# Attention with normalised queries and keys, then a SoLU feed-forward: eleven weight combinations to VectorE, later inner sums, and another way of taking the moments of the last four tiles

## The chip, the cores and the metric

The kernel runs on one core of a Trainium2 chip. The metric is the device time of one execution in microseconds; lower is better. A core has TensorE (PE in the profile, with its weight loads as PEld), VectorE (DVE), ScalarE (ACT), GpSimd (POOL) and SyncE (SP, which here only issues DMAs). Each engine works through its own list of instructions in order, and semaphores make one wait for another.

## The reference

Two blocks follow each other. The attention block takes q, k, v of 8 batches, 12 heads, 448 positions and 64 columns; its result, reshaped to 3584 x 768, is the input x of the feed-forward block.

```python
q_n, k_n = (rmsnorm(q, g_q), rmsnorm(k, g_k))
scores = scale * np.matmul(q_n, k_n.transpose(0, 1, 3, 2))
scores = scores - np.max(scores, axis=-1, keepdims=True)
attn = np.exp(scores)
attn = attn / (np.sum(attn, axis=-1, keepdims=True) + 1e-09)
return np.matmul(attn, v).astype(np.float32)
...
h = x @ w_in
h_max = np.max(h, axis=-1, keepdims=True)
e = np.exp(h - h_max)
sm = e / (np.sum(e, axis=-1, keepdims=True) + 1e-09)
solu = h * sm
mu = np.mean(solu, axis=-1, keepdims=True)
var = np.mean((solu - mu) ** 2, axis=-1, keepdims=True)
ln = (solu - mu) / np.sqrt(var + 1e-06) * g_ln
return (ln @ w_out).astype(np.float32)
```

w_in is 768 x 1024, w_out 1024 x 768. The kernel computes in fp32; the weights reach it as doubles.

## The kernel before

**Three stages.** `fast_path` first runs attention in quads of four heads. Then comes the stage of `w_in`: x in 28 tiles of 128 rows, two tiles to a group `g`, 14 groups. Then the last stage: the normalised result times `w_out`, four tiles to a product, seven products. Both matrix products are made by a scheme of seven half-sized products instead of eight, for which sums and differences of the blocks of both factors are needed; in the last stage the scheme is applied twice, once to halves and once inside each of the seven products.

**The stage of `w_in`.** The seven products of a group are parts `p1` to `p7` (functions in `products`, L1100 the matmul, six matmuls each). They run in the order p6, p5, p7, p4, then p1 of the next group, p3, then p2 of the next group; 98 parts in all. p1, p6 and p7 add up in one PSUM bank, A; p5 and p3 in bank B; p2 has C and p4 has D. `part` (L1107) is ACT's copy of bank A, once after each of p1, p6, p7. `plus` (L1116) is DVE's drain of a bank: it adds ACT's copy, writes a quarter of `h` and carries the row maximum (`top`). So p3 may begin on bank B only when DVE has drained p5's and p7's sum from it, and p7 on bank A only when ACT has copied it.

For the next group POOL makes the block sums: L1076 and L1077 (`block_sums` part 0), then L1079 and L1080 (part 1; L1079 makes the operand of p7). L1076 waits for ACT's L1059 (`sizes`, which uses the same buffer first), and that for DVE's L1048 (`scale`).

**The steps of a tile.** When both halves of a tile's `h` are there (`done`: tile 2g+1 after p4, tile 2g after p3), these steps follow, each put some units of the schedule later (a unit is a part): the exponential on ACT (L1171); `ff_mult`, the product with `h` on DVE, for tiles 0 to 23 by an instruction that also sums the row (L1185, then the mean, L1186); `ff_deviations`, ACT's squares of the deviations from the mean (L1196); `ff_spread_of`, three [128,1] steps on POOL (L1201 to L1204) that end in `shift`; `ff_norm` on ACT (L1224); `ff_spread`, DVE's transpose (L1234) and four DMA stores on SP. For the last four tiles, 24 to 27, `ff_mult` is a plain product (L1180) and `ff_moments` takes mean and variance by batch-norm statistics on DVE (L1212, L1213, three small steps), with two small steps on POOL (L1218, L1220).

**Weights of the last stage.** During the stage of `w_in` the blocks of `w_out` are converted, and 44 subtractions (`combine`, L567, 128x384 each) make the combinations that the scheme needs. All stand on POOL, one per part from part 54 to part 89. They come in chains of four, `t3 = b22 - t1`, `t1 = t1 - b11`, `t2 = b22 - t1`, `t4 = b21 - t2`, so one of a chain may overwrite or read what the one before it touched.

**The seam.** Near the end of the stage the first operands of the last stage are made: tiles 0 to 3 come back from DRAM (`load_u`, SP, L1289), `make` puts them in place (`a11`, `s1`; later `s2`, `a12`, `s3`, ...), and `inner_sums` (four additions on POOL, L1330 to L1333) makes the sums for the inner scheme. PE's matmuls of the last stage are L1352; ACT's and DVE's drains there L1364, L1366, L1391, L1404, L1414.

**What sets the order.** The schedule is written by hand: `unit` emits a part and then what has come due, `follow(parts, i, f)` puts `f` behind part `i`, `later(n, f)` puts it `n` units on. Each engine's instructions stand in the order in which this code emits them.

Of the kernel before, what the change touches and what calls it, by code (L numbers as in the profile page):

```python
# [9 lines left out]
FP32 = mybir.dt.float32  # L10
# [4 lines left out]
OP = AluOpType  # L15
# [351 lines left out]
def fast_path(  # L367
# [24 lines left out]
    nc = tc.nc  # L392
    B, H, S, D = q.shape
    DM, DFF = moe_w_in.shape
    P = 128
# [9 lines left out]
    NG = NT // 2  # L405
# [8 lines left out]
    small = ctx.enter_context(tc.tile_pool(name="small", bufs=4))  # L414
# [8 lines left out]
    w_out = conv = sums_in = None  # L423
# [14 lines left out]
    mhalf = consts.tile([P, 1], FP32, name="mhalf")  # L438
# [121 lines left out]

    def combine(b, i):

        b11, b21, b22, t1, t3, t2, t4 = b
        o, p, q = [(t3, b22, t1), (t1, t1, b11), (t2, b22, t1), (t4, b21, t2)][i]
        nc.gpsimd.tensor_tensor(o, p, q, OP.subtract)  # L567

    def combine_in(x):
        c, i = divmod(x, 4)  # L570
        combine([w_in[k][:, c] for k in range(7)], i)

    def combine_out(x):

        if x < 16:
            k, i = divmod(x, 4)
            combine([w_out[:, a, (0, 3, 1, 2)[k]] for a in range(7)], i)
        else:
            a, i = divmod(x - 16, 4)
            combine([w_out[:, (0, 1, 5, 3, 4, 2, 6)[a], k] for k in range(7)], i)  # L580

    def load_again(x):

# [416 lines left out]
    mt = {}  # L1000
# [161 lines left out]
    def ff_max(t):  # L1162
        d = mt[t]
        d["nmax"] = small.tile([P, 1], FP32, tag="hmax", name="hmax")
        nc.vector.tensor_scalar(d["nmax"], d["top"], -1.0, None, OP.mult)
# [4 lines left out]
        d["s"] = small.tile([P, 1], FP32, tag="hsum", name="hsum")  # L1170
        nc.scalar.activation(d["u"], d["h"], AF.Exp, bias=d["nmax"], accum_out=d["s"])  # L1171

    def two_pass(t):
        return t < 2 * (NG - 2)

    def ff_mult(t):
        d = mt[t]
        u, h = d["u"], d["h"]
        if not two_pass(t):
            nc.vector.tensor_tensor(u, h, u, OP.mult)  # L1180
            return
        x = small.tile([P, 3], FP32, tag="um", name="um")
        total, mean, dev = x[:, 0:1], x[:, 1:2], x[:, 2:3]
        d["mean"], d["dev"] = mean, dev
        nc.vector.tensor_tensor_reduce(u, h, u, 1.0, 0.0, OP.mult, OP.add, total)  # L1185
        nc.vector.tensor_scalar(mean, total, -1.0 / DFF, None, OP.mult)  # L1186
        s = d["s"]
        e = d["e"] = small.tile([P, 1], FP32, tag="he", name="he")
        nc.gpsimd.tensor_scalar(s, s, 1e-9, None, OP.add)
        nc.gpsimd.tensor_scalar(e, s, s, 1e-6, OP.mult, OP.mult)  # L1190
# [7 lines left out]
    def ff_spread_of(t):  # L1198
# [3 lines left out]
        nc.gpsimd.tensor_tensor(e, e, mhalf, OP.pow)  # L1202
        d["shift"] = small.tile([P, 1], FP32, tag="shift", name="shift")
        nc.gpsimd.tensor_tensor(d["shift"], d["mean"], e, OP.mult)  # L1204

    def ff_moments(t):
        d = mt[t]
        u, s = d["u"], d["s"]
        bs = small.tile([P, 2, 6], FP32, tag="bs", name="bs", bufs=2)
        d["mv"] = small.tile([P, 2], FP32, tag="mv", name="mv", bufs=2)  # L1210
        for half in range(2):
            nc.vector.bn_stats(out=bs[:, half], in_=u[:, half * 512 : half * 512 + 512])  # L1212
        nc.vector.bn_aggr(out=d["mv"], in_=bs)  # L1213
        e = d["e"] = small.tile([P, 1], FP32, tag="he", name="he")
        nc.vector.tensor_scalar(s, s, 1e-9, None, OP.add)
        nc.vector.tensor_scalar(e, s, s, 1e-6, OP.mult, OP.mult)
        nc.vector.tensor_tensor(e, e, d["mv"][:, 1:2], OP.add)
        nc.gpsimd.tensor_tensor(e, e, mhalf, OP.pow)  # L1218
        d["shift"] = small.tile([P, 1], FP32, tag="shift", name="shift")
        nc.gpsimd.tensor_scalar(d["shift"], d["mv"][:, 0:1], e, -1.0, OP.mult, OP.mult)  # L1220

    def ff_norm(t):
        d = mt[t]
# [18 lines left out]
    def in_parts():  # L1242
        def done(g, i):
            t = 2 * g + i
            ff_max(t)
            waits = {
                (NG - 2, 1): (1, 2, 4, 6, 6), (NG - 2, 0): (2, 3, 5, 7.25, 8),
                (NG - 1, 1): (1, 2, 3.25, 6.75, 7.25), (NG - 1, 0): (2.25, 4.25, 7, 7.75, 8.75),
            }.get((g, i))
            if two_pass(t):  # L1250
                steps = (ff_exp, ff_mult, ff_deviations, ff_spread_of, ff_norm, ff_spread)
                waits = (1, 2, 3, 4, 5, 7) if i else (2, 3, 4, 6, 7, 9)
            else:
                steps = (ff_exp, ff_mult, ff_moments, ff_norm, ff_spread)
            for x, f in zip(waits, steps):
                later(x, lambda f=f: f(t))

        p = [products(g, lambda i, g=g: done(g, i)) for g in range(NG)]
        parts = [p[0][1], p[0][2]]
        for g in range(NG):  # L1260
            turn = [p[g][6], p[g][5], p[g][7], p[g][4], p[g][3]]
            x = len(parts)
            if g + 1 < NG:
                turn[4:] = [p[g + 1][1], p[g][3], p[g + 1][2]]
            parts += turn
# [55 lines left out]
    def inner_sums(n, name):  # L1321

        own = last.get("u", last["first"])
        a = us[n, name]
        sm = us[n, name, "sums"] = own.tile(
            [P, 4, KC, 4, 32], FP32, tag="sums", name="sums", bufs=2 if own is last["first"] else 4
        )
        a11, a12, a21, a22 = [a[:, t, k * KC : (k + 1) * KC] for t in range(2) for k in range(2)]
        s1, s2, s3, s4 = [sm[:, i] for i in range(4)]
        nc.gpsimd.tensor_tensor(s1, a21, a22, OP.add)  # L1330
        nc.gpsimd.tensor_tensor(s2, s1, a11, OP.subtract)
        nc.gpsimd.tensor_tensor(s3, a11, a21, OP.subtract)
        nc.gpsimd.tensor_tensor(s4, a12, s2, OP.subtract)  # L1333
# [112 lines left out]
    def follow(p, i, f):  # L1446
        g = p[i]

        def both():
            g()  # L1450
            later(1, f)

        p[i] = both
# [61 lines left out]
    with tc.manual_schedule():  # L1515
# [68 lines left out]
        for m in range(1, NQ):  # L1584
            a, b = 2 * m, 2 * m + 1
# [162 lines left out]
        w_out = pool(ctx, "w2", side="right").tile([P, 7, 7, KC, N2], FP32, name="w_out")  # L1748
# [19 lines left out]
        parts = in_parts()  # L1768
# [3 lines left out]
        for x in range(8):  # L1772
            follow(parts, 30 + 2 * x, lambda x=x: combine_out(x))
        for x in range(8, 44):
            follow(parts, 46 + x, lambda x=x: combine_out(x))
        follow(parts, 54, open_first)
        follow(parts, 3, lambda: load_sums(B - 1))
        follow(parts, 6, lambda: (invert(B - 1), send_inverses(B - 1)))
# [1 line left out]
        for name, t, h, i, j in (("a11", 0, (0,), 62, 66), ("a11", 1, (0,), 69, 73), ("s1", 2, (0, 1), 76, 82), ("s1", 3, (0, 1), 83, 89)):  # L1780
            follow(parts, i, lambda t=t, h=h: [load_u(0, t, x) for x in h])
            follow(parts, j, lambda name=name, t=t: make(0, name, t % 2))
        follow(parts, 89, lambda: inner_sums(0, "a11"))
        follow(parts, 93, lambda: inner_sums(0, "s1"))
        for p in parts:
            unit(p)

# [15 lines left out]
        for n in range(NS):  # L1803
            base = period * n
            for i, name in enumerate(ORDER):
                q = len(ORDER) * n + i
# [3 lines left out]
                x = HALVES[name][0]  # L1810
# [118 lines left out]
```

## Time and profile before

| what | before |
|---|---|
| median of 3 runs | 792.34 us (790.93 to 792.76) |
| the profiled execution | 791.55 us |
| its span, first to last instruction | 789.9 us |
| mean granted clock of TensorE | 0.999 |
| w_out subtractions (L567) on POOL | 44, 51.4 us, 1170 ns mean |

The profile is of one execution, so its rows add up to its own 789.9 us, not to the median. It names engines as above, lines of the kernel as L567, and writes an operation as output <- input. An idle time stands in brackets with the engine and line whose end released the instruction. A group of rows gives count, busy time and mean in ns.

### The profile page before, as it was taken

Reading aid. Unit: us, or ns where it says so; the run is one execution under the profiler, and the core shown is the slowest. Engines: PE = TensorE matmul, PEld = TensorE weight load, DVE = VectorE, ACT = ScalarE, POOL = GpSimd, SP = SyncE. Lnnn points to the kernel's source line nnn. Section 1 sums busy time; section 2 is a strip of 40 time slices with the busy share of each in tenths; the row PEclk is TensorE's granted clock in tenths of the full one; section 3 lists DMA queues with packets and bytes.
Section 4 is the critical chain, followed back from the end, with each engine's and each line's share of the span. In section 5 each row is a group of like instructions: output and inputs, shape, how many; then the busy total and the mean of one; then the engine's idle time right before and its main releaser. Section 6 shows DMA issues by size and latency. Waiting matters only on the chain.

```text
span 789.9 us, 15265 instructions
## 1 busy us (share of the span) xinstructions
PE 778.3 (99%) x5374; PEld 481.8 (61%) x5374; DVE 592.8 (75%) x1055; ACT 502.0 (64%) x825; POOL 483.0 (61%) x624
## 2 busy tenths in 40 slices
PE   8999999999999999999999999999999999999997
PEld 4444445444454544444444444443799999999996
DVE  6877997999898883687777666666897685866944
ACT  6776998887979763787777655554526445464410
POOL 2565344454354351455687688899887777867861
PEclk9999999999999999999999999999999999999999
DMA  8889898889898256577786666572757557357312
GB/s 174 177 183 202 172 207 185 187 193 187 169 199 188 77 154 165 141 191 182 186 203 171 166 152 157 138 200 54 210 151 255 162 186 258 127 201 236 105 61 85
DMA packets 279827, 134.28 MB, mean 170 GB/s; under 512 B 190332, under 2 KB 264892, under 8 KB 279740
## 3 DMA queue, kind: packets, MB, share of 16 engines
q1 hardware_dynamic: 265900, 123.31, 62.9%
q10 hardware_dynamic: 13840, 9.90, 4.4%
q8 instruction: 44, 0.72, 0.4%
q14 instruction: 43, 0.35, 0.2%
HBM read 96.12 MB, written 37.04 MB: 169 GB/s over the span
## 4 chain that ended last, share of the span: by engine, by line
PE 86%; POOL 8%; ACT 2%; issue 1%; DVE 1%; DMA 1%; SPq 0%; POOLq 0%; ACTq 0%; DVEq 0%
PE A L1352 16%; PE s L876 15%; PE o L888 15%; PE A L1100 10%; PE B L1352 8%; PE B L1100 6%; PE sm L948 4%; PE C L1352 4%; PE C L1100 3%; PE D L1100 3%; POOL w_out L567 3%; PE pt L790 1%; POOL he L1202 1%; POOL he L1201 1%; POOL xsum L1080 1%
## 5 line engine op out<-in xcount | busy, mean ns | idle before, releaser
L726 POOL TENSOR_TENSOR qkn<-qk,ny 128x896 f32<-128x896 f32 x45 | 77.2, 1735 | 113.9 <-DVE ny L720 82.0
L876 PE MATMUL s<-qkT 64*64 64x448 f32 x1288 | 139.4, 541 | 0.3 <-ACT qkT L742 0.2
L836 ACT ACTIVATE E<-s 128x896 f32<-128x896 f32 x144 | 124.4, 920 | 20.8 <-PE s L876 20.0
L888 PE MATMUL o<-E,v 64*64 64x448 f32 x1104 | 120.4, 536 | 0.0
L876 PEld LDWEIGHTS s<-qkT 64*64 64x64 f32 x1288 | 65.9, 191 | 60.1 <-issue 39.1
L1352 PE MATMUL A<-w_out,sums 128*128 128x192 f32 x392 | 79.9, 326 | 0.3 <-ACT u L1364 0.3
L1352 PE MATMUL B<-w_out,sums 128*128 128x192 f32 x392 | 79.8, 326 | 0.0
L1100 PE MATMUL B<-w_in,xsum 128*128 128x512 f32 x168 | 76.8, 593 | 1.2 <-DVE top L1116 1.2
L1100 PE MATMUL A<-w_in,xg 128*128 128x512 f32 x168 | 76.9, 593 | 0.8 <-POOL xg L1079 0.8
L888 PEld LDWEIGHTS o<-E,v 64*64 64x64 f32 x1104 | 42.3, 133 | 56.2 <-issue 51.5
L1352 PEld LDWEIGHTS A<-w_out,sums 128*128 128x128 f32 x392 | 66.3, 190 | 0.6 <-ACT u L1364 0.6
L1352 PEld LDWEIGHTS B<-w_out,sums 128*128 128x128 f32 x392 | 66.4, 190 | 0.0
L1224 ACT ACTIVATE u<-u,shift,he 128x1024 f32<-128x1024 f32 x28 | 34.8, 1242 | 47.6 <-POOL shift L1204 40.4
L896 DVE TENSOR_TENSOR es<-E 128x896 f32<-128x896 f32 x46 | 57.8, 1257 | 5.8 <-ACT E L836 5.8
L1100 PEld LDWEIGHTS B<-w_in,xsum 128*128 128x128 f32 x168 | 31.8, 190 | 42.0 <-issue 40.3
L1100 PEld LDWEIGHTS A<-w_in,xg 128*128 128x128 f32 x168 | 31.8, 190 | 41.2 <-issue 37.9
L693 DVE TENSOR_REDUCE part<-sq 128x28 f32<-128x896 f32 x46 | 47.9, 1073 | 8.5 <-ACT sq L687 8.5
L567 POOL TENSOR_TENSOR w_out<-w_out 128x384 f32<-128x384 f32 x44 | 51.4, 1170 | 1.4
L747 DVE STREAM_TRANSPOSE qkT<-qkn 128x896 f32<-128x896 f32 x46 | 49.0, 1090 | 3.6 <-POOL qkn L726 3.6
L1076 POOL TENSOR_TENSOR xsum<-xg 128x384 f32<-128x384 f32 x14 | 14.7, 1050 | 59.4 <-ACT xsum L1059 36.3
L1352 PE MATMUL A<-w_out,s 128*128 128x192 f32 x224 | 45.6, 326 | 0.0
L1185 DVE CUSTOM_DVE_ANT_0 u<-h,u 128x1024 f32<-128x1024 f32 x24 | 36.4, 1518 | 11.1 <-ACT u L1171 8.3
(178 smaller groups left out, 1640.8 us busy)
## 6 DMA issues: line engine op xcount, KB each, us to landing
ur<-ud SPq DMA_DIRECT2D x60, 256.0 KB, 4.8
ud<-ub SPq DMA_DIRECT2D x112, 128.0 KB, 2.6
xd<-xo SPq DMA_DIRECT2D x48, 224.0 KB, 3.7
qk<-in_q_dram SPq DMA_DIRECT2D x92, 112.0 KB, 3.7
qk<-in_k_dram SPq DMA_DIRECT2D x92, 112.0 KB, 2.7
v<-in_v_dram SPq DMA_DIRECT2D x23, 448.0 KB, 3.7
out_dram<-P SPq DMA_DIRECT2D x19, 384.0 KB, 3.6
raw<-in_moe_w_in_dram SPq DMA_DIRECT2D x12, 512.0 KB, 4.5
```

The lines of the kernel that those rows point to most:

```text
L567: nc.gpsimd.tensor_tensor(o, p, q, OP.subtract)
L693: nc.vector.tensor_reduce(norms[m]["part"][:, i], st[n]["sq"], AX, OP.add)
L726: e.tensor_tensor(d["qkn"].rearrange("p (s b) d -> p s b d", s=2), d["qk"].rearrange("p s (b d) -> p s b d", d=32), y.rearrange("p (s b) - ...
L747: nc.vector.transpose(d["qkT"].rearrange("p s t -> p (s t)"), d["qkn"].rearrange("p b d -> p (b d)"))
L836: nc.scalar.activation(e, s[:, :, 0:S], AF.Exp)
L876: nc.tensor.matmul(s[i * D : (i + 1) * D, h, 0:S], qkT[hh, i, 1, keys], qkT[hh, i, 0], start=True, stop=True)
L888: nc.tensor.matmul(d["o"][h * D : (h + 1) * D, i, 0:S], d["v"][pp, h, kc], d["E", kc][pp, h], start=kc == 0, stop=kc == NK - 1,)
L896: nc.vector.tensor_tensor(e, d["E", x], d["E", y], OP.add)
L1100: nc.tensor.matmul(k[bank], a[:, c], w_in[i][:, c], start=begin and c == 0, stop=c == HD - 1, skip_group_check=not begin,)
L1185: nc.vector.tensor_tensor_reduce(u, h, u, 1.0, 0.0, OP.mult, OP.add, total)
L1224: nc.scalar.activation(d["u"], d["u"], AF.Identity, scale=d["e"], bias=d["shift"])
L1352: nc.tensor.matmul(k[bank], a[:, c].rearrange("p a i -> p (a i)"), w_out[:, area, i, c], start=begin and c == 0, stop=c == KC - 1, skip_gr ...
```

## The change

Three things are changed, all in `fast_path`.

First, of the 36 subtractions for `w_out` that stand one to a part from part 54 on, those behind parts p4 and p3 of each group go to VectorE: eleven of them. Their order stays, so POOL and DVE now take turns in some chains.

Second, the inner sums of `a11` are emitted behind part 92 instead of 89, those of `s1` behind 94 instead of 93.

Third, `two_pass` and `ff_moments` are removed: the last four tiles take the same six steps as the others, with unit counts of their own.

```diff
-    def combine(b, i):
+    def combine(b, i, e=nc.gpsimd):
...
-        nc.gpsimd.tensor_tensor(o, p, q, OP.subtract)
+        e.tensor_tensor(o, p, q, OP.subtract)
...
-    def two_pass(t):
-        return t < 2 * (NG - 2)
-
     def ff_mult(t):
         d = mt[t]
         u, h = d["u"], d["h"]
-        if not two_pass(t):
-            nc.vector.tensor_tensor(u, h, u, OP.mult)
-            return
...
-    def ff_moments(t):
-        d = mt[t]
-        u, s = d["u"], d["s"]
...
             waits = {
-                (NG - 2, 1): (1, 2, 4, 6, 6), (NG - 2, 0): (2, 3, 5, 7.25, 8),
-                (NG - 1, 1): (1, 2, 3.25, 6.75, 7.25), (NG - 1, 0): (2.25, 4.25, 7, 7.75, 8.75),
-            }.get((g, i))
-            if two_pass(t):
-                steps = (ff_exp, ff_mult, ff_deviations, ff_spread_of, ff_norm, ff_spread)
-                waits = (1, 2, 3, 4, 5, 7) if i else (2, 3, 4, 6, 7, 9)
-            else:
-                steps = (ff_exp, ff_mult, ff_moments, ff_norm, ff_spread)
+                (NG - 2, 1): (1, 2, 3, 4, 5, 6), (NG - 2, 0): (2, 3, 4, 5, 6, 7.25),
+                (NG - 1, 1): (1, 2, 4.5, 5, 7.25, 7.75), (NG - 1, 0): (2.25, 4.25, 5.25, 6, 7.5, 8.75),
+            }.get((g, i), (1, 2, 3, 4, 5, 7) if i else (2, 3, 4, 6, 7, 9))
+            steps = (ff_exp, ff_mult, ff_deviations, ff_spread_of, ff_norm, ff_spread)
...
         for x in range(8, 44):
-            follow(parts, 46 + x, lambda x=x: combine_out(x))
+            e = nc.vector if (44 + x) % 7 in (3, 5) else nc.gpsimd
+            follow(parts, 46 + x, lambda x=x, e=e: combine_out(x, e))
...
-        follow(parts, 89, lambda: inner_sums(0, "a11"))
-        follow(parts, 93, lambda: inner_sums(0, "s1"))
+        follow(parts, 92, lambda: inner_sums(0, "a11"))
+        follow(parts, 94, lambda: inner_sums(0, "s1"))
```

The removed lines move everything below `ff_mult` up: L1224 becomes L1202, L1196 becomes L1190, L1234 becomes L1212, L1289 becomes L1263, L1330 to L1333 become L1304 to L1307, L1352 becomes L1326, L1364 becomes L1338. Lines above, L567 and L1116 among them, keep their numbers.

What now stands on the engines is best seen in their lists. POOL in the last group of the w_in stage, before; the first row is the subtraction behind part 88 (p7), L1201 to L1204 belong to tile 22, the L1330 row opens the inner sums of `a11`, L1079 makes p7's operand of the last group:

```order
L1077 TENSOR_TENSOR xsum<-xsum,xg 128x384
L567 TENSOR_TENSOR w_out<-w_out 128x384
L1201 TENSOR_SCALAR he<-um,he 128x1
L1202 TENSOR_TENSOR he<-he,mhalf 128x1
L1204 TENSOR_TENSOR shift<-um,he 128x1
L567 TENSOR_TENSOR w_out<-w_out 128x384
L1330 TENSOR_TENSOR sums<-a_4995 128x256
...
L1079 TENSOR_TENSOR xg<-xg 128x3x128
L1080 TENSOR_TENSOR xsum<-xg,xsum 128x384
L1218 TENSOR_TENSOR he<-he,mhalf 128x1
L1220 TENSOR_SCALAR shift<-mv,he 128x1
```

And after the change:

```order
L567 TENSOR_TENSOR w_out<-w_out 128x384
L1195 TENSOR_SCALAR he<-um,he 128x1
L1196 TENSOR_TENSOR he<-he,mhalf 128x1
L1198 TENSOR_TENSOR shift<-um,he 128x1
L1183 TENSOR_SCALAR hsum<-hsum 128x1
L1184 TENSOR_SCALAR he<-hsum 128x1
L1079 TENSOR_TENSOR xg<-xg 128x3x128
L1080 TENSOR_TENSOR xsum<-xg,xsum 128x384
...
L1198 TENSOR_TENSOR shift<-um,he 128x1
L1304 TENSOR_TENSOR sums<-a_4995 128x256
```

The subtraction behind the first `shift` is gone from POOL, and the inner sums stand behind L1079, L1080 and the `shift` of tile 25.

DVE at the same place after the change, from the D drain of the last group but one to the product of tile 25; `s_5270` is the operand `s1`:

```order
L1116 ISA h,top<-D,u_5347,top 128x512
L1116 ISA top 128x1
L1165 TENSOR_SCALAR hmax<-top 128x1
L567 TENSOR_TENSOR w_out<-w_out 128x384
L1287 TENSOR_TENSOR s_5270<-ur 128x512
L1179 ISA u,um<-h,u 128x1024
```

The L567 row is new; before, `hmax` was followed by the operand and by the plain product.

ACT from the last copies of bank A in the w_in stage into the last stage, before (`u_5434` and `u_5456` are such copies, `q_5522`, `q_5562`, `u_5566` and `u_5585` copies of the last stage's bank A, `a_5515` is the operand `a12`):

```order
L1107 COPY u_5434<-A 128x512
L1224 ACTIVATE u<-u,shift,he 128x1024
L1107 COPY u_5456<-A 128x512
L1171 ACTIVATE u,hsum<-h,hmax 128x1024
L1364 COPY q_5522<-A 128x192
L1224 ACTIVATE u<-u,shift,he 128x1024
L1171 ACTIVATE u,hsum<-h,hmax 128x1024
L1364 COPY q_5562<-A 128x192
L1364 COPY u_5566<-A 128x192
L1309 COPY a_5515<-ur 128x512 x2
L1364 COPY u_5585<-A 128x192
```

And after, with `u_5432`, `u_5460`, then `q_5524`, `q_5551`, `u_5555`, `u_5579` and `a_5517` in their places:

```order
L1107 COPY u_5432<-A 128x512
L1202 ACTIVATE u<-u,shift,he 128x1024
L1190 ACTIVATE h,um<-u,um 128x1024
L1107 COPY u_5460<-A 128x512
L1202 ACTIVATE u<-u,shift,he 128x1024
L1171 ACTIVATE u,hsum<-h,hmax 128x1024
L1338 COPY q_5524<-A 128x192
...
L1338 COPY u_5555<-A 128x192
L1190 ACTIVATE h,um<-u,um 128x1024
L1283 COPY a_5517<-ur 128x512 x2
L1338 COPY u_5579<-A 128x192
```

The second normalisation (tile 24) moved ahead of the exponential of tile 27, and a square (L1190, tile 27) now stands ahead of the `a12` copies.

More of the change, by code (lines that the diff above doesn't have):

```diff
@@ L571, in combine_in, with combine_out @@
         combine([w_in[k][:, c] for k in range(7)], i)
-    def combine_out(x):
+    def combine_out(x, e=nc.gpsimd):
         if x < 16:
             k, i = divmod(x, 4)
-            combine([w_out[:, a, (0, 3, 1, 2)[k]] for a in range(7)], i)
+            combine([w_out[:, a, (0, 3, 1, 2)[k]] for a in range(7)], i, e)
         else:
             a, i = divmod(x - 16, 4)
-            combine([w_out[:, (0, 1, 5, 3, 4, 2, 6)[a], k] for k in range(7)], i)
+            combine([w_out[:, (0, 1, 5, 3, 4, 2, 6)[a], k] for k in range(7)], i, e)
     def load_again(x):
@@ L1204, in ff_spread_of @@
         nc.gpsimd.tensor_tensor(d["shift"], d["mean"], e, OP.mult)
-    def ff_moments(t):
-        d = mt[t]
-        u, s = d["u"], d["s"]
[L1209 to L1220, printed above, removed]
     def ff_norm(t):
```

## The prediction, made before the changed kernel was run

> **What bounds the kernel now.** First the busy line of the page, then two windows: the seam up to the first matmul of the last stage, and that stage from its eleventh group of matmuls on (columns: busy time of PE, PEld, DVE, ACT, POOL, then clock and DMA).
>
> ```profile
> PE 778.3 (99%) x5374; PEld 481.8 (61%) x5374; DVE 592.8 (75%) x1055; ACT 502.0 (64%) x825; POOL 483.0 (61%) x624
> 518.00:559.19 41.19, 39.16 (x90) 16.57 (x89) 27.13 (x55) 19.27 (x33) 35.83 (x46) 1.00 0.45 115
> 567.32:784.00 216.68, 216.68 (x1336) 216.41 (x1334) 158.50 (x377) 92.19 (x203) 157.60 (x193) 1.00 0.52 172
> ```
>
> PE sets the time: from 567.32 to 784 us it never rests. No matmul is taken away, so the change can win only PE's rests at the seam. The timeline of PE there shows them (start, length, work, idle before and its releaser):
>
> ```profile
> 533.24 2.74 PE L1100 MATMUL D<-w_in,xg 128*128 128x512 f32 x6
> 535.82 2.74 PE L1100 MATMUL A<-w_in,xg 128*128 128x512 f32 x6
> 539.07 2.81 PE L1100 MATMUL B<-w_in,xsum 128*128 128x512 f32 x6 [0.52 <-DVE top L1116]
> ...
> 550.43 2.84 PE L1100 MATMUL A<-w_in,xg 128*128 128x512 f32 x6 [0.81 <-POOL xg L1079]
> ...
> 556.54 2.81 PE L1100 MATMUL B<-w_in,xsum 128*128 128x512 f32 x6 [0.70 <-DVE top L1116]
> 559.19 0.82 PE L1352 MATMUL A<-w_out,a 128*128 128x192 f32 x4
> 559.85 0.81 PE L1352 MATMUL C<-w_out,a 128*128 128x192 f32 x4
> ...
> 563.52 0.92 PE L1352 MATMUL A<-w_out,sums 128*128 128x192 f32 x4 [0.25 <-ACT u L1364]
> ...
> 566.57 0.92 PE L1352 MATMUL A<-w_out,a 128*128 128x192 f32 x4 [0.83 <-ACT u L1364]
> 567.32 0.81 PE L1352 MATMUL B<-w_out,sums 128*128 128x192 f32 x4
> ```
>
> The five idle times add up to 3.11 us. Undisturbed parts start 535.82 - 533.24 = 2.58 us apart (2.575 over many) and groups of four 0.65. From 535.82 come eight parts and ten groups: 535.82 + 20.6 + 6.5 = 562.92, but the eleventh group starts at 567.32. The five rests cost **4.4 us** (start against due start: 0.76, 1.10, 0.94, 0.52, 1.10), 1.3 more than their idle time, since each also breaks the overlap of neighbouring matmuls. That is the most this change can win.
>
> **Why PE rests: POOL falls behind.** POOL's queue empties once per group of two tiles, at L1076, where it waits for ACT's L1059:
>
> ```profile
> 483.30 0.99 POOL L1076 TENSOR_TENSOR xsum<-xg 128x384 f32<-128x384 f32 x1 [1.63 <-ACT xsum L1059]
> 502.76 1.00 POOL L1076 TENSOR_TENSOR xsum<-xg 128x384 f32<-128x384 f32 x1 [1.50 <-ACT xsum L1059]
> 520.81 1.00 POOL L1076 TENSOR_TENSOR xsum<-xg 128x384 f32<-128x384 f32 x1 [0.23 <-ACT xsum L1059]
> 540.08 1.00 POOL L1076 TENSOR_TENSOR xsum<-xg 128x384 f32<-128x384 f32 x1 [0.98 <-ACT xsum L1059]
> ```
>
> These starts are (540.08 - 483.30) / 3 = 18.93 us apart, but PE needs 7 x 2.575 = 18.03 for a group. It is a ring: POOL's work ends in `shift`, ACT's normalisation waits for it and holds ACT's copy and L1059 behind it, and L1059 releases POOL. The ring is 0.9 us per group too slow, and near the end PE feels it (rows of the timelines of ACT, DVE, POOL and SP):
>
> ```profile
> 535.36 1.24 ACT L1224 ACTIVATE u<-u,shift,he 128x1024 f32<-128x1024 f32 x1 [5.02 <-POOL shift L1204]
> 537.63 0.56 ACT L1107 COPY u<-A 128x512 f32<-128x512 f32 x1
> 538.23 0.69 DVE L1116 CUSTOM_DVE_ANT_0 h<-B,u 128x512 f32<-128x512 f32 x1 [3.60 <-ACT u L1107]
> 546.52 0.72 POOL L1330 TENSOR_TENSOR sums<-a 128x256 f32<-128x256 f32 x1
> 549.37 1.00 POOL L1079 TENSOR_TENSOR xg<-xg 128x384 f32<-128x384 f32 x1
> 552.98 0.26 POOL L1220 TENSOR_SCALAR shift<-mv,he 128x1 f32<-128x1 f32 x1
> 553.28 1.24 ACT L1224 ACTIVATE u<-u,shift,he 128x1024 f32<-128x1024 f32 x1 [4.81 <-POOL shift L1220]
> 554.43 0.56 ACT L1107 COPY u<-A 128x512 f32<-128x512 f32 x1
> 554.56 1.25 DVE L1234 STREAM_TRANSPOSE ub<-u 128x1024 f32<-128x1024 f32 x1 [3.03 <-ACT u L1224]
> 557.75 3.93 SPq L1289 DMA_DIRECT2D ur<-ud  x6
> 565.03 1.27 ACT L1309 COPY a<-ur 128x512 f32<-128x512 f32 x2 [1.56 <-DMA ur<-ud]
> 566.20 0.31 ACT L1364 COPY u<-A 128x192 f32<-128x192 f32 x1
> ```
>
> **The change part by part.**
>
> *Eleven of the 44 subtractions go to DVE*, two per group for five groups and one more. From POOL's ring each group loses the one behind `shift` and the one behind L1080:
>
> ```profile
> 492.14 2.03 DVE L1185 CUSTOM_DVE_ANT_0 u<-h,u 128x1024 f32<-128x1024 f32 x1 [0.51 <-POOL xg L1079]
> 493.06 1.97 POOL L567 TENSOR_TENSOR w_out<-w_out 128x384 f32<-128x384 f32 x1
> L1048 DVE TENSOR_TENSOR xg<-xg,rg 128x384 f32<-128x384 f32 x26 | 15.3, 629 | 8.7 <-DMA raw<-in_moe_w_out_dram 4.5 <-DMA rg<-rd 2.9 <-DMA ur<-ud 1.2
> ```
>
> Alone such an operation takes 1.00 (L1076, the same shape); beside L1185 it took 1.97. The ring shortens by 1.00 + 1.97 to 16.0 us. If the second is long only because it meets DVE's L1185, and the next POOL operation inherits that, it shortens by 2.0, to 16.9. Either is under 18.03, so PE leads and POOL waits. The DVE operation is not in this trace; L1048 on the same shape has 0.63 mean, and I take that, with 0.5 (L1116's 0.69 for 512 columns, scaled) and 2.0 (as slow as on POOL) as ends. DVE has the room: 27.1 of 41.2 us are busy. What it can harm stands under the rivals.
>
> Without the lag ACT's copy of the drained bank no longer stands behind `shift`: it starts when its part ends, at 533.3 instead of 537.63, **4.3 us earlier**, and with it L1059, L1076 and DVE's L1116 (538.23 becomes 533.9, needed at 538.4). First rest gone: 0.76.
>
> *Inner sums of `a11` move behind L1079 and L1080.* Before, four operations (546.52 to 549.37) stood ahead of L1079. It would come at 549.37 - 4.3 (lag) - 2.85 (sums) - 1.0 (the last subtraction, now DVE's) = 541.2; PE wants it at 548.7. Even with all the lag it comes at 545.5. Second rest gone: 1.10.
>
> *Moments by deviations for the last four tiles.* The multiply of before in tiles 25 and 27, and the new way as the other 24 tiles have it:
>
> ```profile
> 542.22 1.35 DVE L1180 TENSOR_TENSOR u<-h,u 128x1024 f32<-128x1024 f32 x1 [0.60 <-ACT u L1171]
> 560.60 2.31 DVE L1180 TENSOR_TENSOR u<-h,u 128x1024 f32<-128x1024 f32 x1 [0.26 <-ACT u L1171]
> ...
> L1185 DVE CUSTOM_DVE_ANT_0 u<-h,u 128x1024 f32<-128x1024 f32 x24 | 36.4, 1518 | 11.1 <-ACT u L1171 8.3 <-POOL xg L1079 2.8
> L1186 DVE TENSOR_SCALAR um<-um 128x1 f32<-128x1 f32 x24 | 3.7, 154 | 0.8
> L1196 ACT ACTIVATE h<-u,um 128x1024 f32<-128x1024 f32 x24 | 27.3, 1136 | 0.6 <-DVE um L1186 0.6
> L1196 ACT ACTIVATION_READ_ACCUMULATOR h<-u,um 128x1 f32 x24 | 4.5, 187 | 0.0
> ```
>
> DVE swaps one multiply for another of about the same length and loses L1212 with its small followers; ACT gains 1.14 + 0.19 = 1.3 per tile, POOL three small operations. For tile 25, L1079 to `shift` took 552.98 - 549.37 = 3.6; with one more small operation 4.1, so `shift` comes near 541.2 + 4.1 = 545.3 instead of 552.98. Its square must be done shortly before: POOL's subtraction that DVE waits for (542.45, quoted below) ends near 540 without the lag, then 0.63, an addition of 512 columns (0.84 by L1048), multiply and mean 1.5 to 2.2, square 1.3: about 544, in time. (A subtraction of 2.0 makes it 545.4 and `shift` 546.3, still before ACT comes to it.) ACT then copies at the end of the part at 546.1, normalises tile 25 by 547.9 and squares tile 24 by 549.2; the copy that ran at 554.43 runs when its part ends, at 551.3. Third rest gone: 0.94. Tile 24 is normalised before the last stage, no longer between its copies: fourth rest gone, 0.5.
>
> *The transpose of tile 25* follows near 548 instead of 554.56. Behind it on SP stand four stores and then the six `ur` loads, from 551.2 instead of 557.75. Their data were copied 565.03 - 557.75 = 7.3 after their issue, so they lie ready near 558.5. One further `ur` load passes SP ahead of the stores of tile 27; nothing waits for it soon. The load is no longer last; what is late next is **ACT's queue**: two exponentials, three short copies, now also the square of tile 27, then the two `a` copies and the copy PE waits for. L1100 ends at 535.82 + 20.6 = 556.4. DVE's multiply of tile 27 began 560.60 - 559.19 = 1.4 behind that point before, so now at 557.8; it takes 1.35 to 2.31, its mean 0.15, the square 1.3, the two `a` copies 1.27, the last copy 0.31: 562.2 to 563.1. PE wants it at 556.4 + 9 x 0.65 = 562.3. I take 0.4 lost here and 0.1 at the same place for tile 26.
>
> **Sum.** 0.76 + 1.10 + 0.94 + 0.52 + 1.10 = 4.4, less 0.5: **3.9 us saved**. The profiled execution took 791.55 us (789.9 of span and 1.65 around it), so 787.6; the median of the runs shown is 792.34, 0.8 above it, so **788.4**. Behind the seam PE comes earlier to what the others make, but POOL had an empty queue there soon after:
>
> ```profile
> 577.02 0.73 POOL L1330 TENSOR_TENSOR sums<-s 128x256 f32<-128x256 f32 x1 [1.74 <-DVE s L1319]
> ```
>
> And PE, busy without a break from 567.32 on, had nothing to wait for. I put no loss there.
>
> **Rivals.**
>
> *ACT becomes the bound of the seam.* If both squares, of tiles 27 and 26, hold a copy that PE waits for, each costs up to its 1.3, and 1 to 2.6 us are lost instead of 0.5. For it: the margin above is zero. Against: only slow multiplies bring it about. 1.8 to 3.4 saved: 789 to 790.5.
>
> *The lag stays, and nothing is won.* The load of tile 25 then remains last and other rests come back as they go: 791 to 793.5. Against it stands that the ring would need 2 us per group of new work.
>
> *Slower: DVE now waits in line for POOL.* Four of the six moved subtractions behind DVE's D drain, the last group's among them, read or overwrite what POOL's subtraction behind L1077 touches. DVE then holds everything behind it, among that L1116 for bank B, which the next group's fifth product overwrites four parts, 10.3 us, after the D part's end. From its subtraction to that drain's end DVE needs about 4.5 (0.63, the addition 0.84, a multiply of up to 2.03 with 0.15, the drain 0.69), so PE stalls once POOL's subtraction ends later than 5.8 us after the D part. In the last such group it stood at:
>
> ```profile
> 542.45 1.97 POOL L567 TENSOR_TENSOR w_out<-w_out 128x384 f32<-128x384 f32 x1
> ```
>
> Its end, 544.42, is 8.6 after the D part's (535.8). With the lag of before PE would lose 2.8 us there, and the wait feeds the ring through DVE's mean and ACT's square; with the five rests kept that is 794.4, with the scatter 794 to 796. It decides where the ring is over 18.03. By the rows at 492.14 and 493.06, where both engines took about twice their time, meeting operations cost each other 0.8 to 1.0; if both moved subtractions do that to POOL, the ring is 16.9 + 2 = 18.9 again. The Trainium skill ("SBUF — State Buffer", section "SBUF: two separate sides") says that VectorE operations with two inputs in SBUF and GpSimd operations that read SBUF exclude each other by a lock on a shared port pair for a whole instruction. Those two rows agree. By that rule a moved subtraction still holds POOL for its own length, and the ring gets 16.9 + 2 x 0.63 = 18.2: about PE's pace, the lag growing 0.2 instead of 0.9 per group, which PE would not feel by the end.
>
> **Chances.** Forecast 0.66 (787.2 to 789.2, which takes in the ends of the subtraction and 0 to 0.9 lost behind ACT); ACT as bound 0.16; nothing won 0.09; slower 0.09. Runs of this kernel differ by 0.1 to 0.2% among themselves, and 0.2% (1.6 us) is about what a measurement tells from no change. Faster by more than that takes the forecast and nearly all of the second case: 0.79; same 0.12; slower 0.09. The range runs from the full 4.4 with the scatter of the runs (787.0) into the third case (791.8).
>
> **What will show it.** L1076 of successive groups should start 18.0 us apart and about 2.5 after their part's end; the first three rests are gone; the six `ur` loads issue near 551; the only rest left stands before the tenth group of L1352, 0 to 0.9 us, released by ACT. Wrong if POOL's L1076 starts stay 18.9 apart, or if DVE sits idle before its L567 and PE waits for L1116.

## The result, and the profile after

| | before | after |
|---|---|---|
| median of 6 runs each | 791.97 us (790.93 to 792.80) | 787.08 us (787.03 to 787.46) |
| the profiled execution | 791.55 us | 787.20 us |
| its span | 789.9 us | 785.6 us |
| ratio of the times | | 0.9942 [0.9933, 0.9952] |

The changed kernel is 0.6% faster. (The six runs of the kernel before are the three shown ahead of the prediction and three more.) The busy line of its page, and the engines' shares of the chain that ended last:

```profile
PE 777.3 (99%) x5374; PEld 481.4 (61%) x5374; DVE 596.3 (76%) x1050; ACT 508.3 (65%) x833; POOL 480.1 (61%) x625
PE 97%; DVE 0%; DMA 0%; ACT 0%; POOL 0%; issue 0%; POOLq 0%
```

The busy times have hardly moved; what has gone is waiting. PE's timeline of the seam (start, length, work; an idle time would stand in brackets at the end):

```profile
535.91 2.74 PE L1100 MATMUL A<-w_in,xg 128*128 128x512 f32 x6
538.48 2.74 PE L1100 MATMUL B<-w_in,xsum 128*128 128x512 f32 x6
...
556.51 0.81 PE L1326 MATMUL A<-w_out,a 128*128 128x192 f32 x4
...
562.36 0.86 PE L1326 MATMUL A<-w_out,a 128*128 128x192 f32 x4
563.05 0.81 PE L1326 MATMUL B<-w_out,sums 128*128 128x192 f32 x4
```

The eight parts from 535.91 end at 556.51, 8 x 2.575 later, and the tenth group stands at 556.51 + 9 x 0.65 = 562.36. All five rests are gone; all that is left at the seam is the 0.69 from 562.36 to 563.05, 0.04 more than a group's 0.65.

Why they are gone is read on ACT and POOL. ACT's copies of bank A ahead of L1059 in four successive groups, then one start of L1076:

```profile
479.46 0.59 ACT L1107 COPY u<-A 128x512 f32<-128x512 f32 x1 [1.12 <-PE A L1100]
497.48 0.59 ACT L1107 COPY u<-A 128x512 f32<-128x512 f32 x1 [0.87 <-PE A L1100]
515.51 0.59 ACT L1107 COPY u<-A 128x512 f32<-128x512 f32 x1 [2.17 <-PE A L1100]
533.53 0.59 ACT L1107 COPY u<-A 128x512 f32<-128x512 f32 x1 [1.02 <-PE A L1100]
...
536.00 1.00 POOL L1076 TENSOR_TENSOR xsum<-xg 128x384 f32<-128x384 f32 x1 [0.99 <-ACT xsum L1059]
```

The copies are 18.02 us apart, PE's own pace, and each waits for PE. Before, the last of them stood at 537.63 behind ACT's wait for `shift`. The ring now has 0.9 to 2.2 us to spare, so it is 15.9 to 17.2 us long. The six loads behind tile 25's stores, the last link of the prediction, were issued at 551.37, where 551.2 was forecast:

```profile
551.37 2.93 SPq L1263 DMA_DIRECT2D ur<-ud  x6
```

### The profile page after: what moved, and what is told of

It reads as the page before. It is cut to its first block, busy times and chain, and to the rows that moved or that the text cites. A ratio compares the mean times of both kernels' runs of the same rounds, so it can differ in the third digit from the quotient of the medians.

```text
span 785.6 us, 15267 instructions
## 1 busy us (share of the span) xinstructions
PE 777.3 (99%) x5374; PEld 481.4 (61%) x5374; DVE 596.3 (76%) x1050; ACT 508.3 (65%) x833; POOL 480.1 (61%) x625
## 4 chain that ended last, share of the span: by engine, by line
PE 97%; DVE 0%; DMA 0%; ACT 0%; POOL 0%; issue 0%; POOLq 0%
PE A L1326 16%; PE s L876 15%; PE o L888 15%; PE A L1100 14%; PE B L1100 9%; PE B L1326 8%; PE D L1100 5%; PE C L1100 5%; PE sm L948 5%; PE C L1326 4%; PE pt L790 1%; PE s L846 1%; PE o L933 1%; DMA v<-in_v_dram 0%; DVE part L693 0%; POOL ss L703 0%
## 5 line engine op out<-in xcount | busy, mean ns | idle before, releaser
L1326 PE MATMUL A<-w_out,sums 128*128 128x192 f32 x392 | 79.8, 326 | 0.0
L1326 PE MATMUL B<-w_out,sums 128*128 128x192 f32 x392 | 79.7, 326 | 0.0
L1326 PEld LDWEIGHTS A<-w_out,sums 128*128 128x128 f32 x392 | 66.2, 190 | 0.2 <-issue 0.2
L1326 PEld LDWEIGHTS B<-w_out,sums 128*128 128x128 f32 x392 | 66.4, 190 | 0.0
L1076 POOL TENSOR_TENSOR xsum<-xg 128x384 f32<-128x384 f32 x14 | 14.7, 1053 | 63.9 <-ACT xsum L1059 39.7
L1202 ACT ACTIVATE u<-u,shift,he 128x1024 f32<-128x1024 f32 x28 | 34.8, 1241 | 27.0 <-POOL shift L1198 26.9
L1326 PE MATMUL A<-w_out,s 128*128 128x192 f32 x224 | 45.5, 326 | 0.0
L687 ACT ACTIVATE sq<-qk 128x896 f32<-128x896 f32 x45 | 41.0, 945 | 1.0 <-issue 0.3
L1171 ACT ACTIVATE u<-h,hmax 128x1024 f32<-128x1024 f32 x28 | 32.0, 1141 | 14.5 <-DVE hmax L1165 14.5
```

The source lines that it names most:

```text
L687: nc.scalar.activation(d["sq"].rearrange("p (s b) d -> p s (b d)", s=2), d["qk"], AF.Square)
L1202: nc.scalar.activation(d["u"], d["u"], AF.Identity, scale=d["e"], bias=d["shift"])
L1326: nc.tensor.matmul(k[bank], a[:, c].rearrange("p a i -> p (a i)"), w_out[:, area, i, c], start=begin and c == 0, stop=c == KC - 1, skip_gr ...
```

## Experiments

Each kernel was timed beside the kernel before on the same chip; the four of a table shared one chip and one set of runs of the kernel before. The tables stand for three chips, so kernels of different tables are compared by their distance from their own "before". Kernels made from the kernel before keep its line numbers, the others have those of the changed kernel; where an edit inserts a line, the lines below it count one more.

### One part alone, and all but the subtractions

| kernel | median us | before | ratio |
|---|---|---|---|
| subtractions on DVE only | 788.10 | 791.71 | 0.9952 [0.9939, 0.9964] |
| inner sums later only | 791.08 | 791.71 | 0.9987 [0.9978, 0.9996] |
| moments by deviations only | 792.75 | 791.71 | 1.0011 [1.0002, 1.0020] |
| changed kernel, all subtractions on POOL | 793.43 | 791.71 | 1.0016 [1.0007, 1.0025] |

**Only the subtractions**, in the kernel before (with the new argument `e` of `combine`, as in the change):

```diff
-            follow(parts, 46 + x, lambda x=x: combine_out(x))
+            e = nc.vector if (44 + x) % 7 in (3, 5) else nc.gpsimd
+            follow(parts, 46 + x, lambda x=x, e=e: combine_out(x, e))
```

> The kernel before with only the eleven subtractions given to VectorE. Ring theory (POOL's ring of 18.93 us per group is the cause of most rests, and two subtractions fewer bring it under PE's 18.03): starts of L1076 in successive groups 18.0 us apart instead of 18.9, the first rest gone (0.76); L1079 of the last group comes near 544 (549.37 less 4.3 of lag and 1.0), needed at 548.7, so the second goes too although the inner sums still stand ahead (1.10); the third (0.94) and fifth (1.10) go because shift of tile 25 comes near 548; the fourth (0.52) stays, since tile 24 is still normalised between the copies of the last stage. Saved 3.4 to 3.9 us of 4.4. Rival theory (the order of the last group decides: the inner sums ahead of L1079 and the steps of tiles 24 and 25): at most 1 us saved, rests two to five remain.

3.6 us faster. POOL's first and last step of the last group, and PE's tenth group of the last stage:

```profile
535.77 0.99 POOL L1076 TENSOR_TENSOR xsum<-xg 128x384 f32<-128x384 f32 x1 [1.15 <-ACT xsum L1059]
543.98 1.01 POOL L1079 TENSOR_TENSOR xg<-xg 128x384 f32<-128x384 f32 x1
...
562.35 0.92 PE L1352 MATMUL A<-w_out,a 128*128 128x192 f32 x4
```

L1076 follows its part at once and L1079 starts 4.6 us ahead of the part that needs it (548.55), with the four inner sums still in front of it. No rest is left that the profile names; PE's rows at the seam lose 0.3 us in all. The fourth rest went as well, against what I expected.

**Only the inner sums later**:

```diff
-        follow(parts, 89, lambda: inner_sums(0, "a11"))
-        follow(parts, 93, lambda: inner_sums(0, "s1"))
+        follow(parts, 92, lambda: inner_sums(0, "a11"))
+        follow(parts, 94, lambda: inner_sums(0, "s1"))
```

> The kernel before with only the inner sums moved behind parts 92 and 94. Ring theory: L1076 stays 18.9 apart and the first rest (0.76) stays; L1079 of the last group at about 546.5, so the second rest goes (1.10); shift of tile 25 comes 2.85 earlier, near 550, so the third goes (0.94) and the fifth shrinks from 1.1 to about 0.6, as the loads behind tile 25's stores come 2.85 earlier. Saved 1.8 to 2.8 us. Rival theory (order of the last group decides): over 3 us saved, only the first rest left.

0.6 us, a third of what was expected. The lag stayed and only the second rest, the one for L1079, went. POOL and PE:

```profile
541.12 0.99 POOL L1076 TENSOR_TENSOR xsum<-xg 128x384 f32<-128x384 f32 x1 [0.98 <-ACT xsum L1059]
...
551.21 1.46 POOL L1218 TENSOR_TENSOR he<-he,mhalf 128x1 f32<-128x1 f32 x1 [1.70 <-DVE he L1217]
...
556.33 2.81 PE L1100 MATMUL B<-w_in,xsum 128*128 128x512 f32 x6 [0.53 <-DVE top L1116]
```

L1079 ran at 547.55, in time, but the step after it waited for DVE's statistics of tile 25, which stood behind a transpose that waited for ACT, which had waited for the `shift` of tile 22. The lag reaches the next `shift` on that way too, so the third rest stayed. PE's starts also slip in this execution where they did not in the one of before, by 0.4 us near 531 and by 0.7 near 573 and 578; the first slip lies ahead of the edit, so it is scatter between executions.

**Only the moments**: the changed kernel with `e = nc.gpsimd` and the inner sums behind parts 89 and 93.

> The changed kernel with all subtractions on POOL and the inner sums behind parts 89 and 93, as before: only the moments of tiles 24 to 27 by deviations and their unit counts. Ring theory: L1076 stays 18.9 apart; L1079 still behind the four inner sums near 549.4, shift of tile 25 about 4.1 behind it, near 553.5, so the first three rests and the fifth stay, and only the fourth (0.52) can go: between 0.5 us saved and 0.5 us lost. Rival theory (order of the last group decides): 1.5 us or more saved, the third to fifth rest gone.

1.0 us slower, outside the half microsecond either way that was expected. With the lag the sums and now also two small steps of tile 25 (1.5 us, from 550.15 to 551.66) stand ahead of L1079 on POOL. It starts 2.3 us later than before, and PE rests for it; below, the windows around that rest (busy time of PE, PEld, DVE, ACT, POOL, then the granted clock and DMA):

```profile
550.15 1.07 POOL L1183 TENSOR_SCALAR hsum<-hsum 128x1 f32<-128x1 f32 x1
551.66 0.99 POOL L1079 TENSOR_TENSOR xg<-xg 128x384 f32<-128x384 f32 x1
...
552.71 4.39 PE L1100 MATMUL A<-w_in,xg 128*128 128x512 f32 x6 [2.48 <-POOL xg L1079]
...
552.00:553.50 1.50, 0.79 (x1) 0.50 (x2) 0.00 (x0) 0.00 (x0) 1.50 (x2) 0.65 0.11 22
553.50:555.00 1.50, 1.50 (x3) 0.67 (x2) 0.00 (x0) 0.19 (x1) 1.25 (x5) 0.50 0.00 0
555.00:557.00 2.00, 2.00 (x5) 0.78 (x4) 0.91 (x1) 2.00 (x2) 1.76 (x4) 0.79 0.00 0
```

The part behind the rest took 4.39 instead of 2.74, at half the clock.

**All subtractions on POOL**, the rest of the change kept (`e = nc.gpsimd`).

> The changed kernel with all 44 subtractions on POOL again (inner sums later and moments by deviations kept). Ring theory: L1076 is 18.9 apart again, the first rest (0.76) is back; L1079 near 546.5 is in time; shift of tile 25 near 550.6, the six loads near 555, so up to 1.2 us of rests three to five come back. 1 to 2 us slower than the changed kernel, 3 to 4 us faster than the kernel before. Rival theory (order of the last group decides): within 0.8 us of the changed kernel, 787.1 to 787.9, with at most the first rest back.

Not 3 to 4 us faster than before but slower: two of the three edits together do harm without the first. ACT and PE at the first groups of the last stage, then POOL's last inner sum and the `shift` of tile 24:

```profile
559.94 1.24 ACT L1202 ACTIVATE u<-u,shift,he 128x1024 f32<-128x1024 f32 x1 [4.85 <-POOL shift L1198]
561.09 1.13 ACT L1171 ACTIVATE u<-h,hmax 128x1024 f32<-128x1024 f32 x1
...
562.22 0.29 ACT L1338 COPY q<-A 128x192 f32<-128x192 f32 x1
...
562.66 0.89 PE L1326 MATMUL A<-w_out,sums 128*128 128x192 f32 x4 [1.93 <-POOL hsum L1183]
...
558.01 0.72 POOL L1307 TENSOR_TENSOR sums<-s,sums 128x256 f32<-128x256 f32 x1
...
559.72 0.19 POOL L1198 TENSOR_TENSOR shift<-um,he 128x1 f32<-128x1 f32 x1
```

PE's fourth group adds into the bank that L1338 has to copy first. That copy stood in ACT's list behind tile 24's normalisation, which waited 4.85 us for a `shift` that POOL delivered late: the eight operations of the inner sums, where the second edit puts them, ran from 552.17 to 558.73, directly ahead of the three steps that end in it. (The releaser that PE's row names, a step that ended at 562.63 on POOL, only came last; the copy is what the bank waits for.)

### The same without one of the other parts, and ACT's margin

| kernel | median us | before | ratio |
|---|---|---|---|
| changed kernel | 787.62 | 791.34 | 0.9950 [0.9936, 0.9963] |
| changed kernel, old moments | 788.73 | 791.34 | 0.9964 [0.9951, 0.9978] |
| changed kernel, sums behind 89 and 93 | 787.68 | 791.34 | 0.9952 [0.9938, 0.9965] |
| changed kernel, two copies more on ACT | 788.24 | 791.34 | 0.9963 [0.9949, 0.9976] |

> The changed kernel as it is, timed on the same chip as the three below, so that differences of half a microsecond can be read: 787.0 to 787.6 us, no rest of PE at the seam.

787.62: the middle of this chip's runs is 0.5 above the first measurement, and the gain is 3.7 us here.

**Old moments** (`two_pass`, `ff_moments` and the old unit counts put back):

> The changed kernel with the old moments (batch-norm statistics and the old unit counts) for tiles 24 to 27: subtractions on VectorE and inner sums later only. Ring theory: the first three rests stay away; tile 24 is normalised between the first copies of the last stage again, at most the fourth rest (0.5 us) returns: 0 to 0.6 us slower than the changed kernel. Rival (the new moments carry rests three to five): 1.5 us or more slower, with PE waiting for the copies of the last stage.

1.1 us slower, between the two expectations. ACT and PE:

```profile
561.35 1.21 ACT L1309 COPY a<-ur 128x512 f32<-128x512 f32 x2 [1.11 <-DMA ur<-ud]
...
562.83 0.92 PE L1352 MATMUL A<-w_out,a 128*128 128x192 f32 x4 [0.25 <-ACT u L1364]
```

The fifth rest came back in small: the loads behind tile 25's stores are last again. It makes half of the 1.1 us (0.52 with the group behind it); most of the rest is two small slips, of 0.23 before the seventh group and 0.24 near 574.

**Inner sums as before** (parts 89 and 93):

> The changed kernel with the inner sums of a11 and s1 behind parts 89 and 93 as before. Ring theory: L1079 of the last group comes 2.9 us later, near 545, still before PE wants it (548.8); shift of tile 25 near 548, the six loads near 554, so only the last copy of ACT can be late: 0 to 1 us slower than the changed kernel. Rival (the sums have to be out of L1079's way): PE waits 1 us or more for L1079.

0.06 us, nothing that the medians can tell (in the trace the tenth group is 0.19 late). L1079 starts 3.7 us ahead of the part that needs it (548.58):

```profile
544.83 1.00 POOL L1079 TENSOR_TENSOR xg<-xg 128x384 f32<-128x384 f32 x1
```

**More work on ACT ahead of the copy that was to be late next**:

```diff
         elif name == "a12":
-            nc.scalar.copy(o, in_turn(n, t, 1))
+            for _ in range(3 if (n, t) == (0, 1) else 1):
+                nc.scalar.copy(o, in_turn(n, t, 1))
```

> The changed kernel with the second copy that makes a12 of tile 1 done three times instead of once: 2 x 0.56 = 1.1 us more of ACT just ahead of the copy that PE's tenth group of the last stage waits for. Theory (ACT's queue is next, with 0.1 us to spare): that copy ends 1.1 us later, PE rests about 1.0 us there, released by ACT, and loses 1.0 to 1.4 us in all. Rival (ACT is not near the path there; the 0.1 us is chance): no rest, under 0.4 us slower.

```profile
560.67 2.42 ACT L1284 COPY a<-ur 128x512 f32<-128x512 f32 x4
563.00 0.31 ACT L1339 COPY u<-A 128x192 f32<-128x192 f32 x1
...
563.37 0.92 PE L1327 MATMUL A<-w_out,a 128*128 128x192 f32 x4 [1.08 <-ACT u L1339]
```

The copies took 2.42 instead of 1.12, so 1.30 more; PE rested 1.08. The row is 1.90 behind the one before it, 1.25 over a group's 0.65. ACT is indeed next, with some 0.05 us to spare (1.30 - 1.25). The median rose by 0.62 only, less than the trace's 1.25; the five spans of the changed kernel on this chip differ by 0.7 among themselves.

### The length of the ring

| kernel | median us | before | ratio |
|---|---|---|---|
| changed kernel, L1077 twice | 788.44 | 791.32 | 0.9962 [0.9948, 0.9975] |
| changed kernel, L1077 three times | 792.90 | 791.32 | 1.0015 [1.0006, 1.0024] |
| before, five subtractions on DVE | 788.10 | 791.32 | 0.9956 [0.9943, 0.9970] |
| all subtractions on POOL, tile 24 late | 790.00 | 791.32 | 0.9985 [0.9976, 0.9994] |

```diff
-            nc.gpsimd.tensor_tensor(s2, s1, a11, OP.subtract)
+            for _ in range(2 if g > 7 else 1):
+                nc.gpsimd.tensor_tensor(s2, s1, a11, OP.subtract)
```

> The changed kernel with L1077 (1.33 us on POOL) done twice instead of once for the last six groups. Ring theory: in the changed kernel the copy ahead of L1059 waited 1.0 us for PE in the last group, so the ring is about 17.0 us; with 1.33 it is 18.3, 0.3 above PE's 18.03, so the lag grows by at most 0.3 per group: L1076 18.0 to 18.4 apart, 0 to 0.6 us slower than the changed kernel. Rival (the length of POOL's list is not what counts, only that its operations no longer meet VectorE's): no difference here and none with two repeats.

With one operation more (range 2) L1076 kept PE's pace, with no wait of its own left:

```profile
463.64 1.00 POOL L1076 TENSOR_TENSOR xsum<-xg 128x384 f32<-128x384 f32 x1 [1.45 <-ACT xsum L1059]
...
535.74 1.00 POOL L1076 TENSOR_TENSOR xsum<-xg 128x384 f32<-128x384 f32 x1
```

(535.74 - 463.64) / 4 = 18.03. The seam stayed whole; two rests of 0.32 and 0.22 us came near 576 and 579 and made their groups 0.48 and 0.39 late, where DVE's transpose of tile 26 waited for a later `shift` and held DVE's drains. I had not expected those. Against the changed kernel it lost 0.8 us (788.44 is 2.9 below its before, 787.62 was 3.7 below), a little over the expected 0.6.

> The same with L1077 done three times (2.66 us more of POOL per group). Ring theory: a ring of 19.7 us, lag growing by 1.6 per group over the last six groups; L1076 19.2 to 19.8 apart, rests of PE at the seam and perhaps a group earlier: 4 to 8 us slower than the changed kernel, no faster than the kernel before. VectorE then waits in line for POOL's subtraction behind L1077, as my slower rival had it. Rival: L1076 18.0 apart, under 0.5 us slower.

With two more (range 3) the ring governs. L1076 in the same two groups, then DVE's subtraction and its drain of bank B, ACT's normalisation of tile 24, and PE:

```profile
464.09 0.99 POOL L1076 TENSOR_TENSOR xsum<-xg 128x384 f32<-128x384 f32 x1 [0.37 <-ACT xsum L1059]
...
539.45 1.00 POOL L1076 TENSOR_TENSOR xsum<-xg 128x384 f32<-128x384 f32 x1
...
544.66 0.56 DVE L567 TENSOR_TENSOR w_out<-w_out 128x384 f32<-128x384 f32 x1 [4.48 <-POOL w_out L567]
547.07 0.74 DVE L1117 CUSTOM_DVE_ANT_0 h<-B,u,top 128x512 f32<-128x512 f32 x1
...
559.56 1.24 ACT L1203 ACTIVATE u<-u,shift,he 128x1024 f32<-128x1024 f32 x1 [4.83 <-POOL shift L1199]
...
548.20 2.74 PE L1101 MATMUL B<-w_in,xsum 128*128 128x512 f32 x6
...
562.28 0.89 PE L1327 MATMUL A<-w_out,sums 128*128 128x192 f32 x4 [1.21 <-ACT q L1339]
```

18.84 us apart, a little under the expected 19.2, and the changed kernel is now slower than the kernel before: with the ring over PE's pace nothing is left of the gain. DVE did wait in line for POOL, 4.48 us, but its drain of bank B still ended 0.4 us before PE took the bank at 548.20. What held PE most was ACT, at tile 24's normalisation, as in the kernel with all subtractions on POOL. From 532 on PE's starts slip by 4.5 us in all: 1.4 there, 1.1 ahead of it at ACT's copies of bank A, and 1.8 between 577 and 585 behind DVE's drains. The 1.4 come on a way that the change itself opened, since tile 24's early normalisation is part of it.

**Five subtractions instead of eleven**, in the kernel before: `== 5` in place of `in (3, 5)`.

> The kernel before with only the five subtractions behind p3 of each group given to VectorE. Ring theory (a threshold): one of 1.00 to 1.97 us less per group brings the ring from 18.93 to 17.0 to 17.9, still under 18.03, so L1076 is 18.0 apart and nearly all of the gain of eleven is there: 3 to 4 us faster than the kernel before. Rival (the gain is in proportion to what is moved): 1.5 to 2 us faster, with a lag that still grows.

Five of eleven bring 3.2 us where eleven brought 3.6, far more than in proportion; that fits a threshold. The spacing was only in part as expected. L1076 kept 18.02 up to 500.01; its last two starts are 19.45 and 17.41 apart, the last with no wait of its own, 0.8 us behind PE's pace:

```profile
519.46 0.99 POOL L1076 TENSOR_TENSOR xsum<-xg 128x384 f32<-128x384 f32 x1 [3.30 <-ACT xsum L1059]
...
536.87 1.00 POOL L1076 TENSOR_TENSOR xsum<-xg 128x384 f32<-128x384 f32 x1
```

No rest came of it in the w_in stage. ACT and PE show what is left to the other six, the load and ACT's last copy:

```profile
562.06 1.21 ACT L1309 COPY a<-ur 128x512 f32<-128x512 f32 x2 [1.62 <-DMA ur<-ud]
...
563.54 0.92 PE L1352 MATMUL A<-w_out,a 128*128 128x192 f32 x4 [0.84 <-ACT u L1364]
```

**Tile 24 normalised late**, all subtractions on POOL:

```diff
-                (NG - 2, 1): (1, 2, 3, 4, 5, 6), (NG - 2, 0): (2, 3, 4, 5, 6, 7.25),
+                (NG - 2, 1): (1, 2, 3, 4, 5, 6), (NG - 2, 0): (2, 3, 4, 5, 7.25, 8),
```

> The changed kernel with all subtractions on POOL and tile 24 normalised and transposed at units 7.25 and 8, as before the change, instead of 6 and 7.25. Theory (with the lag, ACT stands before the normalisation of tile 24 and holds its first copy of the last stage, which made the rest of 1.9 us before the fourth group): that copy comes at once, the rest goes, and the kernel is 1 to 2.5 us faster than with the early normalisation: 791 to 792.4. Rival (the place of tile 24 is not the cause; POOL's longer steps are): 793 or more, as with the early normalisation.

790.00 against 793.43 with tile 24 early: 3.4 us by moving two steps of one tile, more than expected (the two ran on different chips, whose kernels before differ by 0.4; each against its own, it is 3.0). ACT's first copy of the last stage waits for PE again, not for `shift`:

```profile
559.41 0.32 ACT L1338 COPY q<-A 128x192 f32<-128x192 f32 x1 [1.28 <-PE A L1326]
```

## Why the prediction was right, point by point

- **PE's rests were the most to win, and POOL's ring the cause.** Right. Shortening the ring alone (only the subtractions) gave nearly all: 3.6 us, where the whole change has 3.7 beside the kernel before on another chip. Lengthening it again by two operations took all of it back. Its length, forecast 16.0 to 16.9 us, is 15.9 to 17.2 by the copies that wait for PE.
- **The subtraction on DVE**, taken as 0.63, measured 0.86 on average, inside its ends of 0.5 and 2.0, and it cost POOL little:

```profile
L567 POOL TENSOR_TENSOR w_out<-w_out 128x384 f32<-128x384 f32 x33 | 37.4, 1135 | 1.4
L567 DVE TENSOR_TENSOR w_out<-w_out 128x384 f32<-128x384 f32 x11 | 9.4, 858 | 11.4 <-POOL w_out L567 11.4
...
525.75 1.01 POOL L1079 TENSOR_TENSOR xg<-xg 128x384 f32<-128x384 f32 x1
...
525.83 1.34 DVE L567 TENSOR_TENSOR w_out<-w_out 128x384 f32<-128x384 f32 x1 [1.65 <-POOL w_out L567]
526.71 1.33 POOL L1080 TENSOR_TENSOR xsum<-xg,xsum 128x384 f32<-128x384 f32 x1
```

  Where both met, the one that began later paid: DVE's took 1.34 instead of 0.55 to 0.68 beside L1079, which kept the 1.01 it takes alone, and then POOL's L1080, begun while DVE's still ran, took 1.33 instead of 1.00. The Trainium skill ("SBUF — State Buffer", section "SBUF: two separate sides") says that such operations exclude each other for a whole instruction; those three rows agree to 0.15 us (526.76, where L1079 ends, and 0.55 would be 527.31; the DVE row ends at 527.17). Its price in the prediction, a ring of 18.2, does not hold: it charged POOL the whole length of DVE's operation, 0.63, where POOL lost 0.33 in a meeting, since DVE did part of the waiting.
- **Which edit takes which rest.** Here the working was off, though the sum was not; with all three edits in place the sum does not depend on which of them takes a rest, so its coming out says nothing for this attribution. I gave the second rest to the later inner sums, the third and fourth to the new moments, and the fifth to the transpose of tile 25 that they bring forward. The subtractions alone left no rest that the profile names; the sums alone took only the second, the moments alone made it longer, and the two together without the subtractions made the kernel slower than before. On top of the subtractions the sums are worth nothing that can be measured (0.06 us), and the moments in place of the old ones 1.1 us with the sums late. Both together add some 0.1 us to the subtractions alone (3.7 against 3.6, on two chips), so with the old moments the later sums seem to cost what the new moments bring back: the subtractions alone gained 3.6, with the later sums 2.6. These two kernels were not timed on one chip, so that is not shown.
- **ACT's queue is next.** Right in place, wrong in size: this is the mis-sized term of the sum. I took 0.5 us lost; ACT's last copy ended at 562.25, the early end of its range of 562.2 to 563.1, and PE lost 0.04 behind it. 1.30 us more of ACT there made a rest of 1.08.
- **The sum.** 4.3 us of span were saved instead of 3.9, so the profiled execution took 787.2 instead of 787.6. The median, 787.08, lies 0.1 below the 787.2 to 789.2 of the forecast case and just inside the whole range, which starts at 787.0. The other 0.9 of the distance to 788.4 is scatter: the median of before was taken 0.8 above its profiled execution, while the changed kernel's lies 0.1 below its own. In the side-by-side runs before spread over 1.9 us and after over 0.4; a reading, not tested, is that the spread sat in the rests.
- **The slower rival.** DVE's wait in line is real (11.4 us in all in the changed kernel, by the row above, and 4.48 once in the kernel with the longest ring), but even there its drain of bank B came in time: 547.81 - 544.66 = 3.15 us from the subtraction to the drain's end, where I had put 4.5. The mechanism that did make a kernel slower than before, the one with all subtractions on POOL, I had not listed: tile 24's early normalisation in front of ACT's first copies of the last stage, when `shift` is late. With the moments alone it was another, the late L1079.

## What to carry to other kernels

Find out first whether an engine off the path is in a ring with the one that bounds, and compare the ring's period with the bound's: over it, every group adds lag; under it, moving more work away brings little more (here five moved subtractions brought 3.2 us, eleven 3.6). An order that hands out steps earlier is only good as long as their inputs come early, so edits of this kind are to be judged together: here the new moments were harmful until the ring was short. The name of the releaser on a wait at the end of such a lag tells where it surfaced, not what caused it.

## What the runs showed of the hardware

In the profiled execution with only the moments, PE rested 2.48 us, and its granted clock was 0.50 from 552.5 to 555.5. It fell while PE still rested, about 2.2 us into the rest (0.94 from 552.0 to 552.5), and the six matmuls behind took 1.65 us more than elsewhere. Rests of 1.93 us (all subtractions on POOL) and 1.21 us (L1077 three times) left the clock of their profiled executions at 1.00. The Trainium skill ("TensorE: Matmul & The Clock Gate", section "HAM oscillation — how this bites in real kernels") puts the gap to avoid at some 3.4 us; this run shows the clock falling in a shorter one.

The drop does not explain why that kernel is slower. Of its eleven executions seven have a mean clock of 0.996, as the profiled one has, and four have 0.998 to 1.000; the four are not shorter (median span 791.65 us against 791.2).
